# A layernorm, long-convolution and Mish MLP kernel: one fused activation in place of Exp, Ln, Tanh and a product, inverse square roots on GpSimd, and extra matmuls

## The chip, the cores and the metric

The kernel runs on one core of a Trainium2 chip. The metric is the device time of one execution in microseconds (us), given as the median of several runs. A core has five engines with their own instruction streams: PE (TensorE, matmuls; PEld is its weight load), DVE (VectorE), ACT (ScalarE), POOL (GpSimd) and SP (SyncE, which here only issues transfers). An engine works through its own stream in order and waits on semaphores for what the others make. Matmuls write to PSUM, and PSUM is emptied ("evicted") by ACT or DVE.

## What is computed

The input `x` is 2048 tokens by 640 channels in bf16. The reference, cut to what matters:

```python
def _layernorm(x, eps=1e-5): return (x - mean(x)) / sqrt(var(x) + eps)

def _A_ref(q, k, v, shift_k, ssm_k, ssm_D):
    k_shift = <4-tap causal filter of k along the tokens, per channel>
    kv = k_shift * v
    y = irfft(rfft(kv, 2S) * rfft(ssm_k, 2S))[:S]      # long convolution, per channel
    y = y + kv * ssm_D
    return q * y

def _B_ref(x, w1, b1, w2):                              # w1: 640 x 1728, w2: 1728 x 640
    h = x @ w1 + b1
    sp = log1p(exp(-abs(h))) + where(h > 0, h, 0)       # softplus(h)
    act = h * tanh(sp)                                  # Mish
    return act @ w2

h  = x + _A_ref(_layernorm(x), k, v, shift_k, ssm_k, ssm_D)
h2 = h + _B_ref(_layernorm(h), w1, b1, w2)
```

The kernel does the transforms of the long convolution as matmuls with tables of sines and cosines. The tokens are cut into 16 tiles of 128 (`t2` in the code), and a tile has one token in each partition.

## The kernel before

The program is written as a list of operations with dependences, engines to choose from and guessed durations; a list scheduler in the kernel puts them in an order, and the instructions are emitted in that order. So a changed operation can also change the places of others. All matmul results go through a ring of four PSUM buffers (`PS = _Ring("ps", 4)`), each 128 x 1024 in fp32.

Up to about 134 us the kernel transforms the inputs and multiplies them in the frequency domain. In that time DVE also takes the first layernorm's statistics, as soon as `x` has come in, and POOL casts the table `t2m` for the last transform. What the change touches comes then. First, the inverse standard deviation of the first layernorm, for all 16 tiles at once, on ACT and then DVE:

```python
    ln1s = OP("ln1s", ("act", 0.3), ln1_ops + [d_small],
              emit=lambda e: nc.scalar.activation(r1v[:], mv1[:, :, 1], ACT.Sqrt, bias=eps_t[:], scale=1.0), prio=45)
    def ln1f_emit(e):
        nc.vector.reciprocal(r1v[:], r1v[:])
        nc.vector.scalar_tensor_tensor(nmr1[:], mv1[:, :, 0], -1.0, r1v[:], ALU.mult, ALU.mult)
```

The first inverse transform (20 groups of 16 matmuls into `ps_i`, evicted into `zb`) runs beside it. Then comes a stage by token tile. For each of the 16 tiles: the second inverse transform (`i2pe`), the first layernorm (`lnx`), the product with it, the residual sum `h`, the statistics of the second layernorm, its standard deviation, a matrix `dR` with the inverse deviation on its diagonal, the centred row `hc`, and a transpose of `hc` by matmuls with `dR`, evicted into `lnhT`:

```python
            for hf in range(2):                                   # i2pe
                for ri in range(2):
                    nc.tensor.matmul(pyv[:, hf, 0:320], PL["t2m_b"][:, t2, ri, :], zb[:, ri, t2, hf * 320:(hf + 1) * 320],
                                     start=(ri == 0), stop=(ri == 1))
            # ... [cut] lnx on ACT; on DVE:
            nc.vector.tensor_tensor(lv, pyv[:, :, 0:320], lv, ALU.mult)                              # wb
            nc.vector.tensor_tensor(XN["xn"][:, t2, :], lnx_rt.tile[:], XN["xn"][:, t2, :], ALU.add)  # h
            # bn_stats x2, bn_aggr -> mv2 (mean, variance)
            nc.scalar.activation(r2[:, t2:t2 + 1], mv2[:, t2, 1:2], ACT.Sqrt, bias=eps_t[:], scale=1.0)
            nc.vector.reciprocal(r2[:, t2:t2 + 1], r2[:, t2:t2 + 1])
            nc.vector.tensor_scalar(PL["dR"][:, t2, :], ident_b[:], r2[:, t2:t2 + 1], None, ALU.mult)
            nc.vector.tensor_scalar(B2["hc"][:, t2, :], XN["xn"][:, t2, :], mv2[:, t2, 0:1], None, ALU.subtract)
            # trpe: 5 matmuls hc x dR -> ps_tr ; trev on ACT, two copies (512 and 128 columns) -> lnhT
```

The MLP takes the tokens in five units, `UNITS = [256, 512, 512, 512, 256]`. The hidden width 1728 is cut into 14 chunks of 128, the last of which has only 64 rows:

```python
        for fc in range(NFC):                                     # 14 chunks
            m = P if fc < 13 else 64
            for dc in range(NDC):                                 # m1pe: 5 matmuls into ps_ph
                nc.tensor.matmul(ph[0:m, 0:w], W["w1s"][:, dc, fc * P:fc * P + m], lnhT[:, dc, c0:c0 + w], ...)
            # hb, on DVE or ACT: ub = ps_ph + b1
            nc.vector.tensor_scalar(hb[0:m, fc, 0:w], rt.tile[0:m, 0:w], b1s[0:m, fc:fc + 1], None, ALU.add)
        # per batch of 7 or 14 chunks:
            nc.scalar.activation(es[:, 0:nfull, :], hb[:, f0:f0 + nfull, 0:w], ACT.Exp)
            nc.scalar.activation(es[:, 0:nfull, :], es[:, 0:nfull, :], ACT.Ln, bias=1.0, scale=1.0)
            nc.scalar.activation(es[:, 0:nfull, :], es[:, 0:nfull, :], ACT.Tanh)
            # ... [cut] the same three for the 64-row chunk
            nc.vector.tensor_tensor(hb[:, f0:f0 + nfull, 0:w], hb[:, f0:f0 + nfull, 0:w], es[:, 0:nfull, :], ALU.mult)
        # per token tile: 2 x 14 matmuls (m2pe) into ps_po, then the residual sum on DVE and a store
                    nc.tensor.matmul(pov[:, hf2, 0:320], hb[0:m, fc, tl * P:(tl + 1) * P],
                                     W["w2s"][0:m, fc, hf2 * 320:(hf2 + 1) * 320], ...)
```

`ub` has room for two units, so the first matmuls of unit `u` wait for the second matmuls of unit `u - 2`. The tiles `es` and `ob` lie in a pool (`poolB`) that opens only when the pool of the tile stage (`poolXI`) has been closed.

Of the kernel before, what the change touches and what calls it, by code (L numbers as in the profile page):

```python
# [9 lines left out]
ALU = mybir.AluOpType  # L10
# [5 lines left out]
D = 640  # L16
# [6 lines left out]
NFC = 14  # L23
EPS = 1e-5
# [177 lines left out]
def kernel(  # L202
# [44 lines left out]
    a12_b = cpool.tile([P, 2, P], BF16, name="a12_b")  # L247
    mask = small.tile([P, 4], F32, name="mask")
    Dn = small.tile([P, NDC], BF16, name="Dn")
    eps_t = small.tile([P, 1], F32, name="eps_t")  # L250
# [24 lines left out]
    R_LNX = _Ring("lnx", 2)  # L275
    R_ES = _Ring("es", 2)
# [23 lines left out]
    def emit_small(e):  # L300
        nc.gpsimd.dma_start(Dn[:], A_ssm_D.rearrange("(c p) -> p c", p=P))
        nc.gpsimd.dma_start(mask[:], dram["mask"])
        nc.gpsimd.dma_start(sk_b[:], A_shift_k.rearrange("(c p) j -> p c j", p=P))
        nc.gpsimd.dma_start(a12_f[:], dram["a12"])
        nc.gpsimd.memset(eps_t[:], EPS)
# [290 lines left out]
    def emit_openXI(e):  # L596
        close_pool("F")
        open_pool("XP", "poolXP", 1)
        XN["xn"] = PL["XP"].tile([P, 16, D], BF16, name="xn")
        open_pool("XI", "poolXI", 2)  # L600
        PL["t2m_b"] = PL["XI"].tile([P, 16, 2, P], BF16, name="t2m_b", bufs=1)
        PL["dR"] = PL["XI"].tile([P, 16, P], BF16, name="dR", bufs=1)
# [58 lines left out]
    d_x = [DMA(f"d_x{hf}", 1.31e6, emit_x(hf), deps=[d_v[1], op_openXI], prio=40) for hf in range(2)]  # L661
    ln1_ops = []
    for t2 in range(16):
        def fn(e, t2=t2):
            for hh in range(2):
# [3 lines left out]
    ln1s = OP("ln1s", ("act", 0.3), ln1_ops + [d_small],  # L669
              emit=lambda e: nc.scalar.activation(r1v[:], mv1[:, :, 1], ACT.Sqrt, bias=eps_t[:], scale=1.0), prio=45)  # L670

    def ln1f_emit(e):
        nc.vector.reciprocal(r1v[:], r1v[:])
        nc.vector.scalar_tensor_tensor(nmr1[:], mv1[:, :, 0], -1.0, r1v[:], ALU.mult, ALU.mult)
    ln1f = OP("ln1f", ("dve", 0.3), [ln1s], emit=ln1f_emit, prio=45)
# [53 lines left out]
    def emit_w(e):  # L729
        wts = big.tile([P, NDC * FF + NFC * D], BF16, name="wts", tag="slot3")  # L730
        wts_rt.tile = wts
        W["w1s"] = wts[:, 0:NDC * FF].rearrange("p (c f) -> p c f", c=NDC)
        W["w2s"] = wts[:, NDC * FF:NDC * FF + NFC * D].rearrange("p (c d) -> p c d", c=NFC)
        nc.sync.dma_start(W["w1s"], B_w1.rearrange("(c p) f -> p c f", p=P))
# [20 lines left out]
    for t2 in range(16):  # L755
        rt = _RT(PS, f"i2_{t2}")

        def pe(e, t2=t2, rt=rt):
# [3 lines left out]
            for hf in range(2):  # L762
                for ri in range(2):
                    nc.tensor.matmul(pyv[:, hf, 0:320], PL["t2m_b"][:, t2, ri, :], zb[:, ri, t2, hf * 320:(hf + 1) * 320],  # L764
                                     start=(ri == 0), stop=(ri == 1))
# [3 lines left out]
        def lnxf(e, t2=t2, lnx_rt=lnx_rt):  # L769
            lnx_rt.tile = PL["XI"].tile([P, D], BF16, name="lnx", tag="lnx")  # L770
# [13 lines left out]
        def bnf(e, t2=t2):  # L784
            for hh in range(2):
# [3 lines left out]
        o_sq = OP(f"ln2s_{t2}", ("act", 0.28), [o_bn],  # L789
                  emit=(lambda e, t2=t2: nc.scalar.activation(r2[:, t2:t2 + 1], mv2[:, t2, 1:2], ACT.Sqrt, bias=eps_t[:], scale=1.0)),  # L790
                  prio=81)

        def drf(e, t2=t2):
            b2_get()
            nc.vector.reciprocal(r2[:, t2:t2 + 1], r2[:, t2:t2 + 1])
            nc.vector.tensor_scalar(PL["dR"][:, t2, :], ident_b[:], r2[:, t2:t2 + 1], None, ALU.mult)
            nc.vector.tensor_scalar(B2["hc"][:, t2, :], XN["xn"][:, t2, :], mv2[:, t2, 0:1], None, ALU.subtract)
        o_dr = OP(f"dr{t2}", ("dve", 0.75), [o_sq], allocs=[b2_rt] if t2 == 0 else (), uses=[b2_rt] if t2 else (), emit=drf, prio=81)
        rtt = _RT(PS, f"tr_{t2}")

        def trpe(e, t2=t2, rtt=rtt):
            pt = ps_alloc(rtt)
            hc = B2["hc"]
            for dc in range(NDC):
                c0 = dc * P if dc < 4 else 512
                nc.tensor.matmul(pt[:, c0:c0 + P], hc[:, t2, dc * P:(dc + 1) * P], PL["dR"][:, t2, :], start=True, stop=True)
        o_trpe = OP(f"trpe{t2}", ("pe", 0.35), [o_dr], allocs=[rtt], uses=[b2_rt], emit=trpe, prio=82)

        def trev(e, t2=t2, rtt=rtt):
            lnhT = B2["lnhT"]  # L810
            pt = rtt.tile
            if e == "act":
                nc.scalar.copy(lnhT[:, 0:4, t2 * P:(t2 + 1) * P], pt[:, 0:512].rearrange("p (c t) -> p c t", c=4))  # L813
                nc.scalar.copy(lnhT[:, 4, t2 * P:(t2 + 1) * P], pt[:, 512:640])
            else:
                nc.vector.tensor_copy(lnhT[:, 0:4, t2 * P:(t2 + 1) * P], pt[:, 0:512].rearrange("p (c t) -> p c t", c=4))
                nc.vector.tensor_copy(lnhT[:, 4, t2 * P:(t2 + 1) * P], pt[:, 512:640])
        o_trev = OP(f"trev{t2}", [("act", 0.9)], [o_trpe], uses=[rtt, b2_rt], emit=trev, prio=82)
        tr_evs.append(o_trev)

    def emit_openB(e):
        close_pool("XI")
        open_pool("B", "poolB", 2)
    op_openB = OP("openB", ("ctl", 0.0), deps=[o for o in ops if o.name.startswith(("p1_", "p2_", "i2pe", "wb", "h", "trpe", "c_t2m", "xe", "lnx", "dr"))],
                  emit=emit_openB, prio=90)
# [13 lines left out]
    for u, w in enumerate(UNITS):  # L839
        c0 = ucol[u]  # L840
        t2s = list(range(c0 // P, (c0 + w) // P))
        hb_ops = {}
        for fc in range(NFC):
            rt = _RT(PS, f"ph{u}_{fc}")
            m = P if fc < 13 else 64

            def pe(e, u=u, fc=fc, rt=rt, m=m, c0=c0, w=w):
                ph = ps_alloc(rt)
                lnhT = B2["lnhT"]
                for dc in range(NDC):  # L850
                    nc.tensor.matmul(ph[0:m, 0:w], W["w1s"][:, dc, fc * P:fc * P + m], lnhT[:, dc, c0:c0 + w],  # L851
# [6 lines left out]
            def hbf(e, u=u, fc=fc, rt=rt, m=m, w=w):  # L858
                hb = hb_of(u)
                if e == "act":  # L860
                    nc.scalar.activation(hb[0:m, fc, 0:w], rt.tile[0:m, 0:w], ACT.Identity, bias=b1s[0:m, fc:fc + 1], scale=1.0)
                else:
                    nc.vector.tensor_scalar(hb[0:m, fc, 0:w], rt.tile[0:m, 0:w], b1s[0:m, fc:fc + 1], None, ALU.add)  # L863
            first = first_hb[0]
            first_hb[0] = False
            o_hb = OP(f"hb{u}_{fc}", [("dve", _dve1(w)), ("act", _act_d(w, True))], [o_pe, c_b1], allocs=[ub_rt] if first else (),
                      uses=[rt] + ([] if first else [ub_rt]), emit=hbf, prio=100 + u)
            hb_ops[fc] = o_hb
        nb = 2 if w == 512 else 1
        per = NFC // nb  # L870
        mul_ops = []
        for b in range(nb):
            f0, f1_ = b * per, (b + 1) * per
            es_rt = _RT(R_ES, f"es{u}_{b}")
            deps = [hb_ops[fc] for fc in range(f0, f1_)]
            has13 = (f1_ == NFC)
            nfull = (f1_ - f0) - (1 if has13 else 0)

            def a1(e, u=u, f0=f0, nfull=nfull, has13=has13, es_rt=es_rt, w=w):
                est = PL["B"].tile([P, 3584], BF16, name="es", tag="es")  # L880
                es_rt.tile = est
                es = est[:].rearrange("p (c x) -> p c x", x=w)
                hb = hb_of(u)
                nc.scalar.activation(es[:, 0:nfull, :], hb[:, f0:f0 + nfull, 0:w], ACT.Exp)  # L884
                if has13:
                    nc.scalar.activation(es[0:64, nfull, :], hb[0:64, 13, 0:w], ACT.Exp)
                nc.scalar.activation(es[:, 0:nfull, :], es[:, 0:nfull, :], ACT.Ln, bias=1.0, scale=1.0)  # L887
                if has13:
                    nc.scalar.activation(es[0:64, nfull, :], es[0:64, nfull, :], ACT.Ln, bias=1.0, scale=1.0)
                nc.scalar.activation(es[:, 0:nfull, :], es[:, 0:nfull, :], ACT.Tanh)  # L890
                if has13:
                    nc.scalar.activation(es[0:64, nfull, :], es[0:64, nfull, :], ACT.Tanh)
            n_el = nfull * w
            dur = 3 * _act_d(n_el) + 2.6 + (3 * _act_d(w) if has13 else 0.0)
            o_a = OP(f"act{u}_{b}", ("act", dur), deps + [op_openB], allocs=[es_rt], uses=[ub_rt], emit=a1, prio=100 + u)

            def mulf(e, u=u, f0=f0, nfull=nfull, has13=has13, es_rt=es_rt, w=w):
                hb = hb_of(u)
                es = es_rt.tile[:].rearrange("p (c x) -> p c x", x=w)
                nc.vector.tensor_tensor(hb[:, f0:f0 + nfull, 0:w], hb[:, f0:f0 + nfull, 0:w], es[:, 0:nfull, :], ALU.mult)  # L900
                if has13:
                    nc.vector.tensor_tensor(hb[0:64, 13, 0:w], hb[0:64, 13, 0:w], es[0:64, nfull, :], ALU.mult)
            o_m = OP(f"mul{u}_{b}", ("dve", _dve2(n_el) + (_dve2(w) if has13 else 0.0)), [o_a], uses=[es_rt, ub_rt], emit=mulf, prio=100 + u)
            mul_ops.append(o_m)
        lasts = []
        for tl, t2 in enumerate(t2s):
            rt = _RT(PS, f"po{t2}")

            def pe2(e, u=u, tl=tl, rt=rt):
# [3 lines left out]
                for hf2 in range(2):  # L913
                    for fc in range(NFC):
                        m = P if fc < 13 else 64
                        nc.tensor.matmul(pov[:, hf2, 0:320], hb[0:m, fc, tl * P:(tl + 1) * P],  # L916
                                         W["w2s"][0:m, fc, hf2 * 320:(hf2 + 1) * 320], start=(fc == 0), stop=(fc == NFC - 1))
            o_pe2 = OP(f"m2pe{t2}", ("pe", 4.3), mul_ops, allocs=[rt], uses=[ub_rt, wts_rt], emit=pe2, prio=100 + u + 0.5)
# [3 lines left out]
            def resf(e, t2=t2, rt=rt, ob_rt=ob_rt):  # L922
                ob_rt.tile = PL["B"].tile([P, D], BF16, name="ob", tag="ob")
# [46 lines left out]
```

## Time and profile before

| what | value |
|---|---|
| device time, median of 4 runs (lowest to highest) | 345.75 us (345.31 to 347.19) |
| span of the profiled execution | 343.4 us |
| busy: PE, ACT, DVE, POOL | 280.2, 236.2, 225.3, 11.6 us |
| mean granted TensorE clock | 0.92 of full speed |

"Busy" is the time in which an engine had at least one instruction in flight, over the whole span. It says little of what a stage is worth: the stages have different limits. The chain of waits does, which follows the work that ended last back through whatever released it. A second thing to read is the row of the granted TensorE clock: in the stage by token tile and once in the MLP it falls to half.

In the views, a line such as `L916` is the line of the kernel; `ps_po<-wts,ub` names what is written and what is read; "idle before" is the time the engine stood idle just before such instructions, with what ended it. A busy time counts each instruction's whole duration, and successive ones overlap a little: DVE's reciprocals last 184 ns each by the group view, but begin only some 75 ns ahead of the next instruction in the timeline.

### The profile page before, as it was taken

To read this page: it belongs to the slowest core of one execution; us is meant where nothing else is said; L and a number is where in the kernel's file an instruction comes from. 1 tells how busy PE (TensorE), PEld (TensorE's weight loads), DVE (VectorE), ACT (ScalarE), POOL (GpSimd) and SP (SyncE) were. 2 spreads that over 40 slices of the span, in tenths; PEclk is the share of its full clock that TensorE was granted. 3 is DMA by queue.
4 is the path that set the end of the run, shared out by engine and by line. 5 is a ranking of instruction groups with operands and counts; after the bars stand their busy time and mean duration, and the time that the engine had idled before them with its cause. 6 is when DMAs were issued, how large, how long until landed. Compare 5 with 4: busy or idle time off the path is not lost.

```text
span 343.4 us, 7771 instructions
## 1 busy us (share of the span) xinstructions
PE 280.2 (82%) x3431; PEld 197.8 (58%) x3438; DVE 225.3 (66%) x385; ACT 236.2 (69%) x243; POOL 11.6 (3%) x25
## 2 busy tenths in 40 slices
PE   0649999989986678996659898799599999907995
PEld 0623889889876578893337543444365564803653
DVE  0456698898979999937999945476344345812411
ACT  1456692469597875795577999999997970799100
POOL 6000000000001400000000000000000000000000
PEclk9965699999999999999557999999999999965999
DMA  6995000000055400008500000000011011000111
GB/s 191 241 381 213 2 2 5 3 2 2 4 196 219 140 4 5 2 2 309 208 1 0 3 0 2 19 19 2 0 38 40 1 39 38 0 0 2 39 40 38
DMA packets 8097, 21.05 MB, mean 61 GB/s; under 512 B 864, under 2 KB 4896, under 8 KB 7264
## 3 DMA queue, kind: packets, MB, share of 16 engines
q1 hardware_dynamic: 7840, 20.42, 17.1%
q8 instruction: 27, 0.44, 0.5%
q0 software_dynamic: 224, 0.14, 0.3%
q14 instruction: 6, 0.05, 0.0%
HBM read 17.94 MB, written 2.62 MB: 60 GB/s over the span
## 4 chain that ended last, share of the span: by engine, by line
PE 41%; ACT 27%; DVE 21%; issue 5%; DMA 4%; SPq 1%; ACTq 0%; DVEq 0%
PE ps_po L916 18%; PE ps_ph L851 7%; ACT es L884 5%; DMA r0s<-tab_r 4%; PE ps_g L370 4%; ACT zb L286 4%; ACT es L887 4%; DVE kvb L576 3%; ACT es L890 3%; PE ps_ks L567 3%; DVE st L666 2%; DVE P L629 2%; DVE lnx L777 2%; ACT b L813 2%; DVE bks L288 2%
## 5 line engine op out<-in xcount | busy, mean ns | idle before, releaser
L916 PE MATMUL ps_po<-wts,ub 128*128 128x320 bf16 x448 | 70.6, 308 | 16.8 <-DVE ub L900 16.8
L916 PEld LDWEIGHTS <-ub 128*128 128x128 bf16 x448 | 42.0, 100 | 46.2 <-DVE ub L900 18.1
L851 PE MATMUL ps_ph<-b,wts 128*128 128x512 bf16 (+3 forms) x343 | 63.6, 343 | 3.1 <-ACT b L813 2.4
L851 PEld LDWEIGHTS <-wts 128*128 128x128 bf16 (+1 forms) x350 | 34.6, 101 | 30.9 <-issue 5.6
L863 DVE TENSOR_SCALAR ub<-ps_ph,b1s 128x512 bf16<-128x512 f32 (+3 forms) x53 | 35.6, 678 | 15.4 <-PE ps_ph L851 14.7
L925 DVE TENSOR_TENSOR ob<-ps_po,xn 128x640 bf16<-128x640 f32 x16 | 13.2, 824 | 49.2 <-PE ps_po L916 49.2
L884 ACT ACTIVATE es<-ub 128x3072 bf16<-128x3072 bf16 (+2 forms) x8 | 23.8, 2970 | 13.4 <-DVE ub L863 13.3
L471 PEld LDWEIGHTS <-G 128*128 128x128 bf16 x512 | 22.2, 96 | 8.1 <-issue 6.3
L623 ACT CAST xb<-ps_s2vs 128x1024 bf16<-128x1024 f32 x20 | 20.2, 1024 | 8.1 <-PE ps_s2vs L489 5.6
L900 DVE TENSOR_TENSOR ub<-ub,es 128x3072 bf16<-128x3072 bf16 (+2 forms) x8 | 15.1, 1888 | 13.9 <-ACT es L890 13.9
L887 ACT ACTIVATE es<-es 128x3072 bf16<-128x3072 bf16 (+2 forms) x8 | 23.8, 2977 | 0.1
L890 ACT ACTIVATE es<-es 128x3072 bf16<-128x3072 bf16 (+2 forms) x8 | 23.8, 2972 | 0.1
L576 DVE TENSOR_TENSOR kvb<-ps_ks,kvin 128x1024 bf16<-128x1024 f32 x10 | 18.6, 1923 | 2.2 <-PE ps_ks L567 2.2
L764 PE MATMUL ps_i<-zb,t2m_b 128*128 128x320 bf16 x64 | 14.5, 382 | 6.8 <-DVE lnx L777 5.9
L771 ACT ACTIVATE lnx<-xn,nmr,r1v 128x640 bf16<-128x640 bf16 x16 | 13.9, 915 | 8.4 <-DVE xn L781 7.0
L712 PE MATMUL ps_i<-a_b,KP 128*128 128x128 bf16 x160 | 18.7, 219 | 1.2 <-ACT zb L286 1.1
L713 PE MATMUL ps_i<-a_b,P 128*128 128x128 bf16 x160 | 18.7, 219 | 0.0
L488 PE MATMUL ps_s2vs<-bvs,G 128*64 128x128 bf16 (+1 forms) x256 | 14.8, 201 | 4.6 <-ACT xb L623 3.6
L567 PE MATMUL ps_ks<-diagm,kT 128*128 128x128 bf16 x320 | 18.4, 219 | 0.1
L567 PEld LDWEIGHTS <-kT 128*128 128x128 bf16 x320 | 17.9, 98 | 0.3 <-DVE kT L288 0.3
L471 PE MATMUL ps_s2v<-bvs,G 128*128 128x128 bf16 (+1 forms) x256 | 13.8, 198 | 5.1 <-DVE KP L636 2.4
L370 PE MATMUL ps_g<-early,sel_b 32*128 32x512 bf16 x32 | 13.8, 624 | 4.4 <-ACT bks L286 4.4
(88 smaller groups left out, 535.2 us busy)
## 6 DMA issues: line engine op xcount, KB each, us to landing
early<-in_A_ssm_k_dram SPq DMA_DIRECT2D x5, 512.0 KB, 8.0
kvin<-in_A_k_dram SPq DMA_DIRECT2D x2, 1280.0 KB, 17.5
kvin<-in_A_v_dram SPq DMA_DIRECT2D x2, 1280.0 KB, 20.7
xn<-in_A_q_dram SPq DMA_DIRECT2D x2, 1280.0 KB, 7.0
out_dram<-ob SPq DMA_DIRECT2D x16, 160.0 KB, 1.8
wts<-in_B_w_dram SPq DMA_DIRECT2D x1, 2160.0 KB, 7.9
wts<-in_B_w_dram SPq DMA_DIRECT2D x1, 2080.0 KB, 14.0
t2m_f<-tab_t2m SPq DMA_DIRECT2D x8, 256.0 KB, 3.0
```

Of the source, the lines that this page charges most:

```text
L370: nc.tensor.matmul(pg[:, c2 * 512:(c2 + 1) * 512], sel_b[:, dl, :], E2["r0b"][:, c * 512:(c + 1) * 512], start=True, stop=True)
L471: nc.tensor.matmul(ps2v[:, fl, :], G[:, f1, :], src[:, f1, d0:d1], start=True, stop=True)
L567: nc.tensor.matmul(pksv[:, tl, :], lhs, PL["diagm"][:, dc * 4 + j, :], start=(j == 0), stop=(j == 3))
L576: nc.vector.tensor_tensor(kvb_rt.tile[:, :, tg * 8:(tg + 1) * 8], pksv.rearrange("p t d -> p d t"), vn[:, tg * 8:(tg + 1) * 8, dc * P:(dc ...
L623: nc.scalar.copy(xb_rt.tile[:].rearrange("p (g f) -> p g f", f=nf), pssr)
L712: nc.tensor.matmul(pzv[:, dgl, :], KP[:, dg, :], a12_b[:, 0, :], start=True, stop=False)
L851: nc.tensor.matmul(ph[0:m, 0:w], W["w1s"][:, dc, fc * P:fc * P + m], lnhT[:, dc, c0:c0 + w], start=(dc == 0), stop=(dc == NDC - 1))
L863: nc.vector.tensor_scalar(hb[0:m, fc, 0:w], rt.tile[0:m, 0:w], b1s[0:m, fc:fc + 1], None, ALU.add)
L884: nc.scalar.activation(es[:, 0:nfull, :], hb[:, f0:f0 + nfull, 0:w], ACT.Exp)
L887: nc.scalar.activation(es[:, 0:nfull, :], es[:, 0:nfull, :], ACT.Ln, bias=1.0, scale=1.0)
L890: nc.scalar.activation(es[:, 0:nfull, :], es[:, 0:nfull, :], ACT.Tanh)
L916: nc.tensor.matmul(pov[:, hf2, 0:320], hb[0:m, fc, tl * P:(tl + 1) * P], W["w2s"][0:m, fc, hf2 * 320:(hf2 + 1) * 320], start=(fc == 0), st ...
```

## The change

It has six parts.

1. The MLP's activation. Bias, Exp, Ln, Tanh and the product become one `Mish` activation per chunk on ACT, straight from PSUM into `ub`. The batches, the tile `es`, the pool `poolB`, and DVE's part in the bias are gone. The second matmuls of a unit wait for its 14 activations.
2. Both inverse square roots go to POOL, as an addition of eps and a power of -0.5, one token tile at a time. ACT's `Sqrt` and DVE's reciprocals are gone.
3. The second layernorm scales while it centres (one `tensor_scalar` with two operations), and the transpose is by the plain identity. `dR` is gone.
4. The transposed tile is evicted by one copy instead of two, for the tiles from 10 on by ACT or DVE.
5. Each half of `i2pe` gets three further matmuls ahead of the two real ones. They read real data and write to the same PSUM half, which the real ones then start over, so their result is not used. They are there to keep TensorE at work in this stage.
6. The hidden width is padded to 14 x 128 = 1792 with zeros (two memsets on POOL), so that the last chunk is like the others; the ring of `lnx` has three buffers instead of two.

```diff
+    def rsqrt_eps(o, v, n):
+        nc.gpsimd.tensor_scalar(o, v, EPS, 0.0, ALU.add, ALU.add)
+        nc.gpsimd.tensor_tensor(o, o, mhalf[:, 0:n], ALU.pow)
-    ln1s = OP("ln1s", ("act", 0.3), ln1_ops + [d_small],
-              emit=lambda e: nc.scalar.activation(r1v[:], mv1[:, :, 1], ACT.Sqrt, bias=eps_t[:], scale=1.0), prio=45)
+    ln1s = [OP(f"ln1s_{g}", ("pool", 0.6 + 0.16 * 1), ... emit=lambda e, g=g: rsqrt_eps(r1v[:, g * 1:(g + 1) * 1], mv1[:, g * 1:(g + 1) * 1, 1], 1)) for g in range(16 // 1)]
-        nc.vector.reciprocal(r1v[:], r1v[:])
... (weights: NDC * FF becomes NDC * FP, FP = NFC * P)
+        nc.gpsimd.memset(W["w1s"][:, :, FF:FP], 0.0)
+        nc.gpsimd.memset(W["w2s"][64:128, 13, :], 0.0)
...
             for hf in range(2):
+                for _ in range(3):
+                    nc.tensor.matmul(pyv[:, hf, 0:320], PL["t2m_b"][:, t2, 0, :], zb[:, 0, t2, hf * 320:(hf + 1) * 320], start=True, stop=True)
                 for ri in range(2):
...
-        o_sq = OP(f"ln2s_{t2}", ("act", 0.28), [o_bn], ... nc.scalar.activation(r2[:, t2:t2 + 1], ..., ACT.Sqrt, ...)
+        o_sq = OP(f"ln2s_{t2}", ("pool", 0.5), [o_bn], prio=81, emit=... rsqrt_eps(r2[:, t2:t2 + 1], mv2[:, t2, 1:2], 1))
-            nc.vector.reciprocal(r2[:, t2:t2 + 1], r2[:, t2:t2 + 1])
-            nc.vector.tensor_scalar(PL["dR"][:, t2, :], ident_b[:], r2[:, t2:t2 + 1], None, ALU.mult)
-            nc.vector.tensor_scalar(B2["hc"][:, t2, :], XN["xn"][:, t2, :], mv2[:, t2, 0:1], None, ALU.subtract)
+            nc.vector.tensor_scalar(B2["hc"][:, t2, :], XN["xn"][:, t2, :], mv2[:, t2, 0:1], r2[:, t2:t2 + 1], ALU.subtract, ALU.mult)
-                nc.tensor.matmul(pt[:, c0:c0 + P], hc[:, t2, dc * P:(dc + 1) * P], PL["dR"][:, t2, :], start=True, stop=True)
+                nc.tensor.matmul(pt[:, c0:c0 + P], hc[:, t2, dc * P:(dc + 1) * P], ident_b[:], start=True, stop=True)
-                nc.scalar.copy(lnhT[:, 0:4, t2 * P:(t2 + 1) * P], pt[:, 0:512].rearrange("p (c t) -> p c t", c=4))
-                nc.scalar.copy(lnhT[:, 4, t2 * P:(t2 + 1) * P], pt[:, 512:640])
+                nc.scalar.copy(lnhT[:, :, t2 * P:(t2 + 1) * P], pt[:, 0:640].rearrange("p (c t) -> p c t", c=5))
...
             def hbf(e, u=u, fc=fc, rt=rt, w=w):
-                hb = hb_of(u)
-                ... (bias add on ACT or DVE)
+                nc.scalar.activation(hb_of(u)[:, fc, 0:w], rt.tile[:, 0:w], ACT.Mish, bias=b1s[:, fc:fc + 1], scale=1.0)
-        nb = 2 if w == 512 else 1
-        ... (the batches: Exp, Ln, Tanh on ACT, the product on DVE)
-            o_pe2 = OP(f"m2pe{t2}", ("pe", 4.3), mul_ops, ...)
+            o_pe2 = OP(f"m2pe{t2}", ("pe", 3.9), hb_ops, ...)
```

## The prediction

> **What bounds the kernel now.** I read the rows of busy time and granted clock first, then the chain of waits, then the groups, then stages of my own choice in a table by windows.
>
> ```profile
> PE 41%; ACT 27%; DVE 21%; issue 5%; DMA 4%; SPq 1%; ACTq 0%; DVEq 0%
> ```
>
> No single engine bounds the span: the chain goes from engine to engine, so I cut it where its engine changes. In the chain in order of time (start, duration, what) the MLP reads:
>
> ```profile
> 201.06 1.28 ACT L884
> 202.36 2.98 ACT es L884
> ...
> 238.85 3.09 ACT es L890
> 241.96 2.04 DVE ub L900
> 244.04 16.96 PE ps_po L916 x112
> 261.00 0.32 PE ps_ph L851
> 261.38 7.40 PE ps_ph L851 x33
> ...
> 309.24 2.04 DVE ub L900
> 311.33 28.20 PE ps_po L916 x168
> 339.55 0.82 DVE ob L925
> ```
>
> From 201 to 242 us it stays on ACT: Exp, Ln and Tanh, each after a table load of 1.28 us. Then comes the product on DVE, then PE, and from 293 to 311 ACT and DVE once more. PE is the engine with the most work here, and it waits for the activation. The table by windows (length, then busy time of PE, PEld, DVE, ACT, POOL, then granted clock) gives what that costs:
>
> ```profile
> 156.40:180.50 24.10, 14.80 (x69) 8.18 (x69) 23.56 (x53) 14.46 (x23) 0.00 (x0) 0.65 0.48 183
> 180.50:201.06 20.56, 18.48 (x153) 13.09 (x155) 17.51 (x77) 17.80 (x55) 0.00 (x0) 0.91 0.00 1
> 201.06:343.40 142.34, 121.28 (x710) 67.50 (x713) 63.91 (x82) 100.59 (x58) 0.00 (x0) 0.95 0.06 19
> ```
>
> In the tile stage (first line) DVE is full at 23.56 of 24.10 us, PE is not, and its clock averages 0.65; in windows of 8 us and less it is 0.50 from 164 to 184. The activation's price by the groups:
>
> ```profile
> L884 ACT ACTIVATE es<-ub 128x3072 bf16<-128x3072 bf16 (+2 forms) x8 | 23.8, 2970 | 13.4 <-DVE ub L863 13.3
> L900 DVE TENSOR_TENSOR ub<-ub,es 128x3072 bf16<-128x3072 bf16 (+2 forms) x8 | 15.1, 1888 | 13.9 <-ACT es L890 13.9
> L863 DVE TENSOR_SCALAR ub<-ps_ph,b1s 128x512 bf16<-128x512 f32 (+3 forms) x53 | 35.6, 678 | 15.4 <-PE ps_ph L851 14.7
> ```
>
> L887 and L890 cost 23.8 us each as well, and the 17 table loads of L884, L887 and L890 3.8 + 10.3 + 7.7 = 21.8 us.
>
> **What the Trainium skill says.** "ScalarE: Activation LUTs", section on the hardware spline evaluator: throughput is one element per cycle and lane whatever the function, 0.833 ns each. The trace agrees for three functions: 3584 elements take 3179 ns as Exp, 3190 as Ln, 3178 as Tanh. Mish is not in the trace; I take the rate of the bias form on ACT. The same page, "What ACT_TABLE_LOAD costs": about 1283 ns and a drain of about 1380. The load is 1283 here; the drain does not show, since the next activation starts 0.01 us after the load. "TensorE: Matmul & The Clock Gate", Part 1: the array runs at half clock unless it has been kept busy. The trace agrees: 0.50 in the tile stage, and 0.50 again from 306 to 314, during and after 10.2 us without a matmul. "SBUF — State Buffer", section on the two separate sides: GpSimd and some DVE instructions exclude each other on a shared port pair. The trace before has little GpSimd work to show it: eight casts, last ones at 0.62 to 0.93 us for the same shape beside a busy DVE.
>
> **The change part by part.** I walked PE's new order through the stages, with durations from this trace.
>
> *Before the tile stage.* ACT loses one table load and a `Sqrt` (1.13 + 0.31 us of the chain at 144.9) and gets a third `lnx` (0.82 us from start to start) ahead of the last evictions: -0.7 us. The tile stage begins at 155.7 instead of 156.4. The 16 small inverse roots on POOL run beside DVE's statistics and end with them.
>
> *Tile stage.* DVE's intervals from start to start in the timeline, per tile: product 0.735, sum 0.40, statistics 0.79 + 0.11, reciprocal 0.075, `hc` 0.28, `dR` 0.155, together 2.545; times 16 is 40.7 us, which is what the timeline has (156.9 to 197.3). The change takes out 0.23 per tile: 37.0 us. PE gets 10 matmuls of 320 columns per tile instead of 4. At full clock one takes 0.151 us (16.96 / 112 in the chain), so a tile takes 1.51 and 16 take 24.2 us. DVE's part that a tile's buffer waits for is 1.135 us and some statistics in between, about 1.36. So PE becomes the bound of the first half, keeps busy, and should keep its full clock. It ends at 179.9 (before: about 175.8 at half clock). Ten transposes (0.55) and two evictions with a first transpose in front (1.5) bring the first MLP matmul to 182.0, where it was 180.5: the extra matmuls cost 1.5 us here.
>
> *Start of the MLP.* The new order on PE is: 11 chunks of unit 0, transposes 2 to 9, the last 3 chunks, two chunks of unit 1, second matmuls of tile 0. A chunk of 256 columns at full clock is 0.548 us by the spacing of its evictions: 11 end at 188.0. DVE, after the last product at 181.8, has 13 statistics, 7 aggregates and 8 `hc`: 5.1 + 0.8 + 2.2 = 8.1, so until 189.9; PE gets `hc` in time. ACT then evicts eight transposes, some 0.6 each (512 columns take 0.48 from start to start, 1024 take 0.93): until about 193.6. Three Mish follow, 0.4 each, while PE does two chunks of 1.1. Tile 0's second matmuls start at 195.7, on a warm PE.
>
> *The rest.* From there PE should never wait long. ACT needs some 0.6 us for a Mish of 512 columns (706 ns in the bias form, less the overlap) and PE 1.106 for the chunk (7.78 and 7.70 us per 35 matmuls), and every unit's last Mish hides under the next unit's first chunk. What is left for PE: 448 second matmuls x 0.151 = 67.7; 40 chunks of 512 x 1.106 = 44.2; 14 chunks of 256 x 0.548 = 7.7; the last transposes 1.7 and 0.4 of waiting in the buffer ring; 0.7 for unit 4's last Mish, which nothing covers. Sum 122.4: PE ends at 318.1. Before, PE ended at 339.5 and the span 3.85 us later: 322. The device time lies 1.9 to 2.4 above the span (345.31 with this profile, median 345.75): **324.5 us**, 21 us less, a ratio of 0.939. Padding adds nothing on PE, as a matmul's time goes by its columns (311 ns for 64 rows, 308 for 128); the weights land near 170 and are wanted at 182.
>
> So the gain is where PE waits: the stretch from 201.06 lost 142.3 - 121.3 = 21 us of PE, and some more at half clock.
>
> **The rivals.** *GpSimd becomes the bound.* A power of one element per partition is not in the trace. If a pair took 2 us, the first 16 would end about 10 us late, of which the wait for `lnx` shows perhaps 4; the second 16 would arrive in time for tiles 0 to 9 and late for the rest. If such an instruction also held the port against DVE, up to 32 x 1 us could come on top. Against it: a POOL memset takes 0.1 to 0.2 us, a cast of 512 elements 0.62. It would make the time 328 to 340. *The extra matmuls cost more than they bring.* They add 14.5 us of PE work in a stage where PE had spare time. If the clock falls all the same, the stage takes 16 x 2.86 = 46 us, and the time is about 346: no gain. For it: the clock fell in this stage before; against it: PE had gaps of 0.8 to 1.6 us per pair of tiles there, and will have none. *Mish is slow on ACT.* Up to 1.1 us per chunk is hidden; at 1.5 us, 42 chunks cost 17 us more: 341. *ACT between two function tables:* in the built order only two table loads remain, so this one is out. *Clock at full load:* PE will be busy 120 us on end; the trace has 54 us on end at 1.00. A few per cent less would be 4 to 6 us.
>
> **Range and chances.** Small waits that the walk skips cost more often than they gain: 319 to 333. Over 2% faster means below 338.8; only the second and third rival, or a very slow power, come near. Faster 0.95, within 2% 0.03, slower 0.02.
>
> **What would show it.** Right: PEclk at 9 through the tile stage; no wait of PE over 1 us after 196; L916's share of the chain up, nearly all PE; two table loads; POOL's groups under 0.5 us each; first MLP matmul near 182. Wrong: DVE or ACT waiting for POOL, a Mish of 512 columns over 1.1 us, the clock at half between 160 and 185, or PE waiting for `ub`.

## The result and the profile after

| | before | predicted | after |
|---|---|---|---|
| device time, median | 345.41 us | 324.5 us | **311.52 us** (310.31 to 313.61) |
| ratio to before, measured side by side | | 0.939 | **0.9023**, 95% interval 0.8994 to 0.9052 |
| span of the profiled execution | 343.4 us | 322 us | 310.1 us |
| first MLP matmul | 180.5 | 182.0 | 178.0 |
| first second matmul (of tile 0) | 244.0 | 195.7 | 192.4 |
| PE's last matmul ends | 339.5 | 318.1 | 306.2 |

The kernel became faster as foretold, but by 34 us and not by 21, and the range of 319 to 333 us did not hold it. Where the gain lies is as predicted: compare the third column with the fourth. What does not fit is the size of the terms, above all the time of one matmul of 320 columns.

The shares of the chain of waits in the kernel after, by engine:

```profile
PE 60%; DVE 19%; ACT 9%; DMA 5%; issue 4%; SPq 1%; POOL 0%; ACTq 0%; DVEq 0%
```

PE had 41% before and ACT 27%. From the tile stage on, the chain in order of time (start, duration, what) reads:

```profile
155.80 0.57 PE ps_i L768 x3
...
176.41 1.56 DVE lnx L783 x2
177.99 6.18 PE ps_ph L846 x55
...
192.44 3.82 PE ps_po L870 x28
...
216.17 15.21 PE ps_po L870 x112
...
298.59 7.62 PE ps_po L870 x56
306.23 0.82 DVE ob L879
```

L768 is an extra matmul of the tile stage, L783 the product on DVE, L846 the first and L870 the second matmul of the MLP (L851 and L916 before). Through the tile stage the chain runs on DVE. From 192 us on it is PE, but for two sums on DVE of 0.8 us each; the 41 us of Exp, Ln and Tanh that stood ahead of 244 are gone. The line to look at twice is the one of 112 matmuls: 15.21 us, where the same 112 took 16.96 before. The prediction has nothing that makes a second matmul faster, and yet each takes 0.136 us instead of 0.151.

A group of the kernel before and three of the kernel after (busy us, mean ns of one, then idle time before with its cause):

```profile
L916 PE MATMUL ps_po<-wts,ub 128*128 128x320 bf16 x448 | 70.6, 308 | 16.8 <-DVE ub L900 16.8
L870 PE MATMUL ps_po<-wts,ub 128*128 128x320 bf16 x448 | 61.8, 299 | 0.0
L854 ACT ACTIVATE ub<-ps_ph,b1s 128x512 bf16<-128x512 f32 (+1 forms) x70 | 41.6, 605 | 67.7 <-PE ps_ph L846 66.3
L663 POOL TENSOR_TENSOR r<-r,mhalf 128x1 f32<-128x1 f32 x16 | 9.9, 616 | 1.3
```

PE no longer waits for `ub`: the 16.8 us ahead of L916 are 0.0 ahead of L870. ACT now waits for PE (66.3 us ahead of L854), so the wait has turned round. The mean of 605 ns mixes two shapes; by form a Mish of 512 columns takes 687 ns, and PE needs over a microsecond for the chunk. The power on POOL takes 616 ns, more than I allowed, but DVE waits for it only 0.5 us in the whole run.

By stage (length, then busy time of PE, PEld, DVE, ACT, POOL, then granted clock):

```profile
155.80:177.99 22.19, 21.09 (x161) 15.31 (x161) 21.22 (x43) 12.85 (x16) 3.18 (x6) 1.00 0.54 196
177.99:192.44 14.45, 13.40 (x121) 10.24 (x122) 14.45 (x48) 12.79 (x24) 9.29 (x24) 1.00 0.01 2
192.44:310.10 117.66, 113.34 (x743) 71.80 (x746) 17.55 (x26) 36.66 (x58) 2.05 (x3) 1.00 0.07 23
```

The clock is 1.00 in all three; before it was 0.65, 0.91 and 0.95. In the last stage PE is busy for 113.3 of 117.7 us, and most of the rest is the last tile's sum and store.

### The profile page after: what moved, and what is told of

It reads as the page before. It is cut to its first block, busy times and chain, and to the rows that moved or that the text cites. A ratio compares the mean times of both kernels' runs of the same rounds, so it can differ in the third digit from the quotient of the medians.

```text
span 310.1 us, 7914 instructions
## 1 busy us (share of the span) xinstructions
PE 273.6 (88%) x3527; PEld 206.7 (67%) x3534; DVE 173.6 (56%) x289; ACT 165.0 (53%) x204; POOL 43.7 (14%) x91
## 4 chain that ended last, share of the span: by engine, by line
PE 60%; DVE 19%; ACT 9%; DMA 5%; issue 4%; SPq 1%; POOL 0%; ACTq 0%; DVEq 0%
PE ps_po L870 20%; PE ps_ph L846 20%; DMA r0s<-tab_r 5%; PE ps_g L370 4%; DVE kvb L576 4%; PE ps_ks L567 4%; DVE lnx L783 3%; ACT zb L286 2%; DVE bks L288 2%; PE ps_s2k L471 2%; PE ps_s2vs L488 2%; ACT xb L622 2%; DVE P L628 2%; DVE xn L787 2%; PE ps_s2v L471 2%
## 5 line engine op out<-in xcount | busy, mean ns | idle before, releaser
L854 ACT ACTIVATE ub<-ps_ph,b1s 128x512 bf16<-128x512 f32 (+1 forms) x70 | 41.6, 605 | 67.7 <-PE ps_ph L846 66.3
L846 PE MATMUL ps_ph<-b,wts 128*128 128x512 bf16 (+1 forms) x343 | 61.4, 335 | 1.6 <-DVE lnx L783 1.1
L870 PE MATMUL ps_po<-wts,ub 128*128 128x320 bf16 x448 | 61.8, 299 | 0.0
L870 PEld LDWEIGHTS <-ub 128*128 128x128 bf16 x448 | 43.8, 98 | 17.3
L846 PEld LDWEIGHTS <-wts 128*128 128x128 bf16 x350 | 34.2, 98 | 27.5 <-issue 1.5
L768 PE MATMUL ps_i<-zb,t2m_b 128*128 128x320 bf16 x96 | 18.2, 299 | 0.2
L429 PE MATMUL ps_k<-ident_b,early 128*128 128x128 bf16 x80 | 7.3, 270 | 11.3 <-DVE early L417 11.3
L286 ACT CAST zb<-ps_i 128x1024 bf16<-128x1024 f32 x16 | 15.5, 1022 | 1.9 <-PE ps_i L715 1.7
L715 PEld LDWEIGHTS <-P 128*128 128x128 bf16 x160 | 15.6, 98 | 0.6 <-issue 0.6
L714 PEld LDWEIGHTS <-KP 128*128 128x128 bf16 x160 | 15.6, 98 | 0.0
```

Of the source, the lines that this page charges most:

```text
L286: nc.scalar.copy(o, i)
L714: nc.tensor.matmul(pzv[:, dgl, :], KP[:, dg, :], a12_b[:, 0, :], start=True, stop=False)
L715: nc.tensor.matmul(pzv[:, dgl, :], P2[:, dg, :], a12_b[:, 1, :], start=False, stop=True)
L846: nc.tensor.matmul(ph[:, 0:w], W["w1s"][:, dc, fc * P:(fc + 1) * P], lnhT[:, dc, c0:c0 + w], start=(dc == 0), stop=(dc == NDC - 1))
L854: nc.scalar.activation(hb_of(u)[:, fc, 0:w], rt.tile[:, 0:w], ACT.Mish, bias=b1s[:, fc:fc + 1], scale=1.0)
L870: nc.tensor.matmul(pov[:, hf2, 0:320], hb[:, fc, tl * P:(tl + 1) * P], W["w2s"][:, fc, hf2 * 320:(hf2 + 1) * 320], start=(fc == 0), stop=( ...
```

## The experiments

My theory after the result had three parts: (a) the unexplained 15 ns of a second matmul come from the padding, that is, from the 64-row chunk that is gone; (b) the extra matmuls hold the clock and so are worth more than they cost; (c) Mish takes ACT out of PE's way, and the power on GpSimd is what makes that possible, since `Sqrt` needs another function table. The rivals: the matmuls go faster because of what runs beside them and not because of the rows, the extra matmuls bring nothing, and the table loads would be hidden anyway. Each time is the median of all runs; one run of four each of no_extra (321.09 us) and old_act (328.84 us) was in a slower state, which lifts these two medians by 0.15 and 1.2 us.

### The 64-row chunk

**rows64.** The kernel after, with the last chunk of each second matmul on its 64 real rows again. The left-out rows are zero, so the result is the same.

```diff
                     for fc in range(NFC):
+                        m = P if fc < 13 else 64
-                        nc.tensor.matmul(pov[:, hf2, 0:320], hb[:, fc, ...], W["w2s"][:, fc, ...], ...)
+                        nc.tensor.matmul(pov[:, hf2, 0:320], hb[0:m, fc, ...], W["w2s"][0:m, fc, ...], ...)
```

> The changed kernel, but the last chunk of the second matmuls uses its 64 real rows again; all else as after the change. Theory A (a 64-row matmul among 128-row ones stalls TensorE): in the trace before, the start spacing round such a matmul is 232, 239 and 146 ns where it is 136 elsewhere, 0.21 us each; 32 of them are 6.7 us, all on PE's path: 318.2 us. Theory B (the wider mean spacing before came from its surroundings, from ACT's and DVE's batches at the same time, and not from the rows): no change, 311.5 us.

Measured: 319.14 us, ratio 0.9235 (0.917 to 0.930). A holds. The chain has 16.78 us for 112 second matmuls again. The group view by form, the 64-row matmul and its weight load:

```profile
L871 PE MATMUL ps_po<-wts,ub 64*128 64x320 bf16 x32 | 9.8, 307 | 0.0
L871 PEld LDWEIGHTS <-ub 64*128 64x128 bf16 x32 | 3.0, 93 | 8.4 <-issue 8.4
```

The mean of one matmul, 307 ns beside 300 for the others, hides the cost, and that is what misled me. It stands in the second line: PEld is idle for 8.4 us ahead of the 32 loads, 0.26 us for each, and "issue" says that it waits for nothing that the profile shows. On PE the same can be seen in the spacing of starts. In the trace of the kernel before, second matmuls start 136 ns apart, but 232 before a 64-row one, 239 after it, and 146 after the next.

**rows64_pair.** The same, but the second half of a tile takes its 64-row chunk first, so that the last of one half and the first of the next stand side by side.

```diff
+                    fcs = list(range(NFC)) if hf2 == 0 else [13] + list(range(13))
```

> As rows64, but the second half of each tile takes its 64-row chunk first, so that the two 64-row matmuls of a tile stand side by side: still 32 of them, half as many switches of row count. If the switch between row counts costs (A1): 16 x (96 + 103 + 10 ns) = 3.3 us over the changed kernel, 314.9 us. If each 64-row weight load costs by itself (A2): as rows64, 318.2 us. Theory B: 311.5 us.

Measured: 315.02 us, ratio 0.9124 (0.9063 to 0.9186). It is the switch between 128 and 64 rows that costs, not a 64-row matmul as such: the same number of 64-row loads, and half the switches.

```profile
L872 PE MATMUL ps_po<-wts,ub 64*128 64x320 bf16 x32 | 7.1, 301 | 0.0
L872 PEld LDWEIGHTS <-ub 64*128 64x128 bf16 x32 | 1.8, 94 | 4.2 <-issue 4.2
```

The idle time ahead of the loads is halved, from 8.4 to 4.2 us. By the chain, 112 matmuls take 16.78 us with 8 lone chunks, 16.05 with 4 pairs and 15.21 with none: 0.20 us for a lone chunk, 0.21 for a pair.

**pad_only.** The other way round: the kernel before with the padding alone.

```diff
-            m = P if fc < 13 else 64
+            m = P
-            has13 = (f1_ == NFC)
+            has13 = False
```

> The kernel before with the padding of the hidden width alone (128 rows and columns in the last chunk, zero weights). Theory A: of the 448 second matmuls 392 lie on the chain that sets the end, so 28 of the 32 stalls are taken off it: 5.9 us faster, 339.5 us. Theory B: unchanged, 345.4 us.

Measured: 334.08 us, ratio 0.9681 (0.9604 to 0.9758): more than A expected. Its second matmuls:

```profile
L919 PE MATMUL ps_po<-wts,ub 128*128 128x320 bf16 x448 | 65.9, 311 | 10.2 <-DVE ub L903 10.2
```

Their busy time falls by 4.7 us (from 70.6), and the wait for the product falls from 16.8 to 10.2. The second part was not in my expectation: without the 64-row chunk the batches also lose their separate small activations (0.30 and 0.52 us each in the chain of the kernel before), and the scheduler orders units and batches in another way. How the second part divides between these two was not tried.

### The extra matmuls and the clock

**no_extra.** The kernel after without its 96 extra matmuls, whose result is never used.

```diff
-                for _ in range(3):
+                for _ in range(0):
```

> The changed kernel without the 96 extra matmuls. Theory C (they keep the clock up, and that pays): granted clock 0.5 in most of the tile stage and for some 4 us of the MLP, whose matmuls of that time take twice as long: 2 to 4 us slower, 313.5 to 315.5 us. Theory D (the tile stage is bound by DVE either way and the extra matmuls bring nothing): 309.5 to 311.5 us.

Measured: 316.37 us, ratio 0.9159 (0.9088 to 0.923). The extra matmuls do pay, but the loss is larger than C had it. Two stretches by windows, and one line of DVE's timeline, whose bracket is the idle time before:

```profile
170.00:178.00 8.00, 1.08 (x7) 0.42 (x5) 7.35 (x16) 3.57 (x4) 0.76 (x2) 0.79 0.00 0
178.00:186.00 8.00, 5.80 (x36) 4.31 (x37) 7.29 (x25) 4.47 (x7) 5.25 (x15) 0.57 0.00 0
```

```profile
178.07 0.45 DVE L801 TENSOR_SCALAR b<-xn,mv,r 128x640 bf16<-128x640 bf16 x1 [0.72 <-POOL r L663]
```

The clock is at 0.57 as the MLP starts, but PE is also nearly empty from 170 to 178 (1.08 of 8 us). The third line tells why: taking matmuls out changed the scheduler's order on DVE, and the normalised rows of tiles 0 and 1 (L801) now come only after all 16 products. In the kernel after they stand between the products of tiles 8 to 10. The first MLP matmul is at 181.6 instead of 178.0. So this run has two causes in one.

**no_extra_early.** To part them: no extra matmuls, and the operations that normalise tiles 0 and 1 put back by hand to an early place in the order.

```diff
+    for t, before in ((0, 8), (1, 9)):
+        moved = [o for o in order if o.name in (f"ln2_{t}", f"ln2s_{t}", f"dr{t}")]
+        order = [o for o in order if o not in moved]
+        at = next(i for i, o in enumerate(order) if o.name == f"wb{before}")
+        order[at:at] = moved
```

> The kernel after without its 96 extra matmuls, as in no_extra (316.4 us), but with one thing put right that moved there by itself: the normalisation of tiles 0 and 1 is put ahead of the last tiles' work on DVE, as it stands in the kernel after. Theory F (the loss of 4.9 us in no_extra is partly the order on DVE, 3.6 us of later first MLP matmuls, and partly the clock, 1.6 us in the first 55 of them): the first MLP matmul comes before 179 us, the clock is still near 0.5 to 0.65 as the MLP starts, and the time is 312.5 to 314. Theory G (the clock is all that matters, the order follows from it): it stays at 315.5 to 317.

**extra3_pull.** The same order with the three extra matmuls per half, so that they are the one edit between the two.

> The kernel after with all of its extra matmuls and the same forced place on DVE for the normalisation of tiles 0 and 1 as in no_extra_early: beside that run it has the extra matmuls as its one difference. If the extra matmuls are worth the clock alone, no_extra_early is slower than this by 1 to 2 us; if they are worth 4 to 5 us whatever the order, by that. Against the kernel after (311.5) I expect 310.5 to 312.5: the same.

**extra1_pull.** The same with one extra matmul per half.

> As extra3_pull (312.2 us), with one extra matmul per half of a tile in place of three; no_extra_early has none (314.1 us). If one extra is enough to hold the clock through the tile stage: 311.5 to 312.5 us, and the granted clock 1.0 from 160 to 186. If the clock needs PE full: about 313 to 314.5 us, with the clock under 0.9 in part of that stretch.

| kernel | extra matmuls per half | us | ratio to before (interval) |
|---|---|---|---|
| no_extra_early | 0 | 314.06 | 0.908 (0.9028 to 0.9131) |
| extra1_pull | 1 | 313.73 | 0.9105 (0.9033 to 0.9177) |
| extra3_pull | 3 | 312.19 | 0.9023 (0.8961 to 0.9084) |

F holds, at the upper edge of its range: with the order put right, 2.3 of no_extra's 4.9 us are gone. What is left for the clock is about 2 us, the three intervals overlap, and it is the traces that show the cause. The same two stretches of no_extra_early:

```profile
170.00:178.00 8.00, 5.03 (x24) 2.92 (x24) 7.69 (x15) 5.40 (x8) 0.79 (x2) 0.51 0.00 0
178.00:186.00 8.00, 8.00 (x49) 6.11 (x48) 8.00 (x28) 5.02 (x10) 5.49 (x14) 0.64 0.00 1
```

of extra1_pull:

```profile
170.00:178.00 8.00, 6.09 (x30) 3.80 (x30) 7.69 (x15) 5.41 (x8) 0.79 (x2) 0.61 0.00 0
178.00:186.00 8.00, 6.19 (x59) 5.33 (x58) 8.00 (x28) 5.99 (x12) 5.44 (x14) 1.00 0.01 3
```

and of extra3_pull:

```profile
170.00:178.00 8.00, 7.13 (x59) 5.23 (x57) 7.69 (x17) 4.97 (x7) 1.34 (x3) 1.00 0.01 2
178.00:186.00 8.00, 6.93 (x65) 5.83 (x64) 8.00 (x27) 6.64 (x14) 5.23 (x13) 1.00 0.00 1
```

The last figure but two is the clock: 0.51 and 0.64 with none, 0.61 and 1.00 with one, 1.00 throughout with three. At the low clock the first 55 MLP matmuls take 9.10 us in no_extra_early's chain, against 6.18 in the kernel after. At the first second matmul 1.5 us of this are left (194.49 against 192.95 us in extra3_pull). One extra matmul is not enough to hold the clock: PE stands idle for 3.04 us ahead of 170.62, waiting for DVE, the clock is low after it, and from 186 to 190 us it averages 0.57 once more. By the ratios the run with one is no faster than the run with none.

### Mish, the power and the function tables

**mish_only.** The kernel before with Mish in place of bias, Exp, Ln, Tanh and product; nothing else.

```diff
-                nc.vector.tensor_scalar(hb[0:m, fc, 0:w], rt.tile[0:m, 0:w], b1s[0:m, fc:fc + 1], None, ALU.add)
+                nc.scalar.activation(hb[0:m, fc, 0:w], rt.tile[0:m, 0:w], ACT.Mish, bias=b1s[0:m, fc:fc + 1], scale=1.0)
-        ... (the batches)
```

> The kernel before with Mish alone in place of Exp, Ln, Tanh and the product: no padding, no extra matmuls, and Sqrt stays on ACT, so that its instruction order on ACT goes to and fro between Sqrt and Mish, with some 17 table loads of 1.28 us where the kernel after has 2. Theory H (the loads are paid, since PE waits for the activations while they happen): about 14 x 1.28 = 18 us of ACT in the way at the start of the MLP, of which a part lies beside the tile stage, and the 64-row switches of 6.7 us stay: 325 to 335 us. Theory I (the loads lie beside PE's work): 311.5 + 6.7, and up to 2 for the clock: 317 to 320 us.

Measured: 344.45 us, ratio 0.995 (0.9931 to 0.997). Both theories missed: alone, the part that I took for the heart of the change gains half a per cent. H had the right mechanism and made it too small. The table loads by group, and a piece of the chain (L790 is `Sqrt`, L860 is Mish; 1.28 is a load):

```profile
L860 ACT ACT_TABLE_LOAD x8 | 10.3, 1283 | 0.1
L790 ACT ACT_TABLE_LOAD x7 | 9.0, 1283 | 0.1
```

```profile
184.30 1.28 ACT L790
185.59 0.30 ACT r L790
185.91 1.28 ACT L860
187.20 0.47 ACT ub L860
```

ACT takes the `Sqrt` of one tile, then a Mish, then a `Sqrt`, and loads a table each time: 0.8 us of work for 2.6 us of loads. The chain stays on ACT for nearly all of 184 to 218 us, and 14 of the 15 loads (19.2 us) are on it, so they do not lie beside other work, and the second matmuls begin at 218.7.

**mish_pow.** The same with the inverse roots as a power on GpSimd. The operations keep the place and duration that the scheduler assumed for `Sqrt`, to hold the order close to mish_only's.

```diff
-        ... nc.scalar.activation(r2[:, t2:t2 + 1], mv2[:, t2, 1:2], ACT.Sqrt, bias=eps_t[:], scale=1.0)
+        ... rsqrt_eps(r2[:, t2:t2 + 1], mv2[:, t2, 1:2], 1)
-            nc.vector.reciprocal(r2[:, t2:t2 + 1], r2[:, t2:t2 + 1])
```

> mish_only (344.5 us) with the inverse roots as a power on GpSimd in place of Sqrt on ACT: two table loads are left, no padding, no extra matmuls, the factor still in the diagonal of the transposes. Theory H (mish_only gained almost nothing because ACT went to and fro between two tables at the start of the MLP): the 26 us by which its second matmuls begin later go nearly all, and what stays over the kernel after is 6.7 for the rows, 2 to 3 for the clock, and 2 to 4 for the order and the longer work on DVE: 321 to 326 us. Theory L (the loads were in the shadow, something else in mish_only was slow): over 335 us.

Measured: 324.48 us, ratio 0.9416 (0.9327 to 0.9504). H holds. Two loads are left, and the second matmuls, in its chain, begin 20.4 us earlier than in mish_only:

```profile
198.34 8.50 PE ps_po L877 x56
```

The times differ by 20.0 us. From there to PE's end both kernels take 120.4 us, where the kernel after takes 113.8: the 6.6 us are the row switches, and the other 5.9 us that it is behind the kernel after lie ahead of 198.34 (clock, order, more work on DVE).

**pow_only.** The kernel before with the power alone.

> The kernel before with the power on GpSimd alone; Exp, Ln, Tanh and the product stay. Theory M (the power is worth its place only together with Mish, as the table loads of the three functions stay, 17 of the 19): -0.5 for one Sqrt load, a little for DVE's reciprocals: 342 to 346 us. Theory N (old_act at 323.7 us was lower than padding alone at 334.1 by 10.4, and most of that is the power, which takes waits between DVE and ACT out of the tile stage): 334 to 339 us.

Measured: 343.48 us, ratio 0.9938 (0.9912 to 0.9964). M holds: 17 of the 19 table loads stay. So neither of the two gains much, 2.2 and 2.7 us, and both together gain 21.7.

**old_act.** From the other end: the kernel after with Exp, Ln, Tanh and product instead of Mish; padding, power and extra matmuls stay.

```diff
-                nc.scalar.activation(hb_of(u)[:, fc, 0:w], rt.tile[:, 0:w], ACT.Mish, bias=b1s[:, fc:fc + 1], scale=1.0)
+                hb = ub: bias on DVE or ACT; then per batch Exp, Ln, Tanh and the product, as before, without a 64-row part
```

> The kernel after with Exp, Ln, Tanh and the product in DVE in place of Mish; padding, extra matmuls and the power on GpSimd stay. Theory J (the activation was what PE waited for, and is the larger half of the gain): as pad_only (334.1 us) less up to 4 for the clock and the order of the tile stage: 329 to 334 us, with a wait of over 8 us of PE for the product. Theory K (the padding and the clock are the gain and Mish only shortens ACT's own time): under 318 us.

Measured: 323.65 us, ratio 0.9333 (0.9263 to 0.9403). Neither J nor K. Its chain and its wait of PE for the product:

```profile
197.21 1.28 ACT L886
198.50 3.19 ACT es L886
...
255.14 2.03 DVE ub L894
...
261.28 15.21 PE ps_po L907 x112
```

```profile
L907 PE MATMUL ps_po<-wts,ub 128*128 128x320 bf16 x448 | 63.5, 304 | 3.7 <-DVE ub L894 3.7
```

The chain stays on ACT from 190 to 255 us, with ten loads on it, so it looks as if the activation were in the way throughout. But the group says that PE waits for the product only 3.7 us: since ACT lags, PE meanwhile does first matmuls of later units, whose buffers are free. Between 178 us and its end PE is idle for 11.1 us by windows, against 1.5 in the kernel after. So the kernel without Mish is 11 to 12 us slower, and J had overrated it. Not all of this is the activation: another 4.0 us of PE's idle time is a wait for DVE's normalised rows (L802) ahead of a transpose.

```profile
189.92 4.75 PE L811 MATMUL ps_tr<-ident_b,b 128*128 128x128 bf16 x50 [3.96 <-DVE b L802]
```

In the kernel after, the transposes that follow the first matmuls start at 184.7 us. Here the scheduler put the statistics of more tiles ahead of those rows on DVE, so this run, like no_extra, has two causes in one; no run parts them. Against pad_only the span of old_act is 8.1 us shorter: its first MLP matmul is 2.1 us earlier, PE's idle time after it 2.0 less, and PE's busy time for the same matmuls 3.9 less, at a clock of 0.91 to 0.99 instead of 0.92 to 0.96. Which of the parts that it has over pad_only (power, extra matmuls, shorter DVE work, one eviction for two) brought how much was not tried.

## Why the prediction missed

The mechanism was right: PE waited for the activation, and with Mish it does not. **The step that failed is the term of 0.151 us for a matmul of 320 columns, and behind it one sentence: "Padding adds nothing on PE, as a matmul's time goes by its columns (311 ns for 64 rows, 308 for 128)."** The kernel after takes 0.136 us. The two lengths in the sentence are right, and padding adds no cost; what the sentence passes over is that padding takes a cost away. The lengths are those of single matmuls, and these overlap; the time of a stream goes by the spacing of starts. The padding was counted at zero, and it is worth about 6.5 us of PE in the kernel after (32 x 0.20 us = 6.3; from the first second matmul to PE's end rows64 takes 120.4 us and the kernel after 113.8). The 0.151 us that I multiplied by 448 came from a stretch that had eight 64-row chunks in it, so it carried the cost over to a kernel that has none.

Term by term, the span is 11.9 us below the predicted 322:

- *The rest* (192.4 to 306.2): 113.8 us instead of 122.4. The 448 second matmuls take 0.1358 us each instead of 0.151: -6.8. The 40 chunks of 512 columns take 1.079 us by the timeline (14.03 us for 13) instead of 1.106: -1.1; before, every unit had a narrower last chunk, around which the spacing rose from 216 to 310 and 240 ns. Smaller waits make -0.7.
- *Tile stage*: the first MLP matmul is 4.0 us early. The 160 matmuls were also counted at 0.151: -2.4. The first tile's matmuls start at 154.0, ahead of the 155.7 from which I counted, and two short waits between the first tiles take some back: about -1.3. Transposes and evictions: -0.2. PE is near full with its clock at 1.00, as predicted, but it is not the bound alone. At 0.136 us ten matmuls take 1.36 us per tile, and DVE takes 1.33 (16 products and what stands between them from 156.75 to 177.97). The chain runs on DVE, and PE's first MLP matmul waits 1.09 us for DVE's last product:

```profile
177.99 6.16 PE L846 MATMUL ps_ph<-b,wts 128*128 128x256 bf16 x55 [1.09 <-DVE lnx L783]
```

ACT's two evictions, which the walk of the prediction followed, end at 177.94 us, almost at the same time.

- *"Extra matmuls cost 1.5 us here"* was too much, by the same 0.151: DVE's work ends the stage nearly as late without them. By extra3_pull against no_extra_early they put off the first MLP matmul by 0.4 us (178.2 against 177.8), and win 2.9 us in the 55 matmuls after it, 1.5 in all at the first second matmul; the full clock there was in the prediction.
- *Start of the MLP*: 14.45 us instead of 13.7, walked rightly. Of the 51.6 us gained at the first second matmul 18 are given back later, as PE still has the first matmuls ahead of it that it did meanwhile before; the sum of PE's work in the prediction had that too.
- *Before the tile stage*: 155.8 against 155.7.
- The device time lies 1.4 above the span and not 2.5: the last 1.1 us.

The Trainium skill would have given the right term. "TensorE: Matmul & The Clock Gate", Part 1, has the start-to-start time of warm matmuls as the columns at 2.4 GHz plus about 2.5 ns; for 320 columns that is an estimate of 135.8 ns, and the trace after has 136. The 151 ns that I measured before was 11% above that, and the difference should have been asked about.

**Of the rivals**, GpSimd as the bound is out: the pair of addition and power takes 0.86 us from start to start, longer than my "under 0.5 us each" allowed, but DVE loses 0.5 us to it, and two statistics and an aggregate on DVE take 0.86 us beside it and took 0.90 before. Mish is not slow. The clock holds over 120 us of dense work (1.00 in all three stages). "Extra matmuls cost more than they bring" is out by extra3_pull. The two function tables were struck out for the kernel after, rightly; mish_only shows how large that danger was, 20 us.

## What to carry to other kernels

The cost of one instruction in a stream is the spacing of starts in an undisturbed stretch, and when a mean is above that, look for the odd ones: one odd shape in 14 cost 11% here. Here the fused activation paid only once nothing else on ACT needed another table in between (2.2 us alone, 21.7 with the power); look at the built order for functions that go to and fro before counting its gain. When an experiment takes instructions out, compare the orders of the other engines first, or the run measures the scheduler as well.

## What the hardware showed that I had not expected

- A lone 64-row matmul between 128-row ones costs 0.20 us of PE (1.57 us for 8), two side by side cost 0.21 together, and PEld's idle time before the 64-row load is 0.26 us. Zeros that keep all chunks at 128 rows cost nothing that can be seen.
- The granted clock falls to half without a long gap on PE. "TensorE: Matmul & The Clock Gate", Part 1, "HAM oscillation — how this bites in real kernels", names idle gaps of over 3.4 us as what to avoid; in the tile stage of the kernel before, the clock is at 0.50 from 164 us on, and up to then no gap is above 1.62 us. Here the measurement decides: gaps under 3.4 us can be enough. They need not be: in no_extra_early a gap of 1.63 us ahead of 163.52 leaves the clock at 1.00, and it falls with one of 3.31 us ahead of 170.56. No run here shows a threshold.
- A power of one element per partition takes GpSimd 0.56 to 0.98 us, and an addition mostly 0.23, at most 0.78, in the kernel after.
